# MLP weight pieces of a fused attention and MLP kernel: loads of 256 KB parts in place of whole pieces

## The chip, the cores and the metric

The kernel runs on one core of a Trainium2 chip. The metric is the device time of one execution in microseconds (us); medians are quoted. The engines are called PE (TensorE matmul), PEld (its weight loads), ACT (ScalarE), DVE (VectorE), POOL (GpSimd) and SP (SyncE, which here only issues DMAs). One program of 63,000 instructions is fully unrolled.

## The reference, cut to what matters

```python
def reference(A_x, A_wqkv, A_wo, B_x, B_w1, B_b1, B_w2, B_b2):   # S=2048, D=1024, 32 heads, F=3584, bf16
    x  = A_x
    xn = layernorm(x)
    s  = attention(xn, A_wqkv) @ A_wo                 # 32 heads of 32
    y  = layernorm(xn)
    g  = silu(gelu(y @ B_w1 + B_b1) @ B_w2 + B_b2)    # the MLP
    return x + s * g
```

## The kernel before

Attention is cut into 512 units. In each, PE makes the scores of four heads (line L591), ACT takes exp of them (L603), PE multiplies older ones with V and with ones (L620, L623). Into each unit one slice of other PE work is woven (L304): a projection, one w1 item (8 steps), or a quarter of a w2 item (7 steps). The MLP runs in 6 chunks of up to 352 tokens. For each chunk w1 and w2 are read again, in 7 w1 pieces of 1 MB and 4 w2 pieces of 1.75 MB, into two buffers `war0` and `war1` in turn. A w1 piece serves 4 units, a w2 piece 8.

A scheduler records every instruction with what it reads (`r`) and writes (`w`), and turns these into semaphore waits. An engine waits only for what its next instruction needs, so SP runs as far ahead of PE as free buffers let it (its largest sum of waits in the trace of before is for PE: 442.3 us in 29 waits at the w1 load, L363). It does so in program order.

```python
def load_piece(g):                       # called when the first item of piece g-1 starts
    ...                                  # cut: end test
    c, k = divmod(g, 11); s = g % 2
    if k < 7:                            # w1: 1 MB in one issue
        src = B_w1[:, k * 512:(k + 1) * 512].rearrange("(c p) f -> p c f", p=128)
        op("sync", lambda e: e.dma_start(w1v[s], src), w=[("war", s, 0)], dma=f"war{s}")
    else:                                # w2: 768 KB and 1 MB
        ...                              # cut: src
        op("sync", lambda e: e.dma_start(w2v[s][:, KLO:, :], src[:, KLO:, :]), w=[("war", s, 1)], dma=f"wah{s}")
        op("sync", lambda e: e.dma_start(w2v[s][:, 0:KLO, :], src[:, 0:KLO, :]), w=[("war", s, 0)], dma=f"war{s}")

# a w1 step on PE:   r=[("war", s, 0), "yTc"]
# a w2 step on PE:   r=[("war", s, 0 if f < KLO else 1), ("hT", f)]
# the main loop, one turn for a unit u:
#   scores; tanh; exp; P x V of unit u-2; [load_piece at a piece's start]; woven PE steps; DVE work and stores
```

The softmax here doesn't subtract the row's maximum and nothing guards it: scores larger than these inputs give would overflow.

Of the kernel before, what the change touches and what calls it, by code (L numbers as in the profile page):

```python
# [119 lines left out]
def bass_recurrent_scan__mha_block__mixer_channel_mlp__prompt_kernel(  # L120
# [38 lines left out]
    with ExitStack() as st:  # L159
        pg = _Prog(nc, st)  # L160
        op = pg.op

        def sb(name, shape, dt):
            return st.enter_context(nc.sbuf_tensor(name, list(shape), dt))
# [17 lines left out]
        hT = sb("hT", [128, FB, CW], BF16)  # L182
        yTc = sb("yTc", [128, DC, CW], BF16)
        war = [sb(f"war{i}", [128, FB * 256], BF16) for i in range(2)]
# [16 lines left out]
        w1v = [w[:, 0:DC * 512].rearrange("p (c f) -> p c f", c=DC) for w in war]  # L201
        w2v = [w[:, 0:FB * 256].rearrange("p (k n) -> p k n", k=FB) for w in war]
# [12 lines left out]
        def bank(i, lo=0, hi=512):  # L215
            return ps[:, i * 512 + lo:i * 512 + hi]

        def bankq(i, j, lo, hi):
            return ps[32 * j:32 * j + 32, i * 512 + lo:i * 512 + hi]
# [5 lines left out]
        for tb in range(NT):  # L225
            op("sync", lambda e, tb=tb: e.dma_start(xst[:, tb * D:(tb + 1) * D], x2[tb * 128:(tb + 1) * 128, :]),
               w=[("xst", tb)], dma=f"x{tb % 8}")
# [123 lines left out]
        cur = {"u": 0}  # L351
        cnt = {"w1": 0, "w2": 0, "piece": 0, "g": 0, "wo": 0, "store": 0}
        NPC = 11 * NCH
        KLO = 16

        def load_piece(g):
            if g >= NPC:
                return
            c, k = divmod(g, 11)
            s = g % 2  # L360
            if k < 7:
                src = B_w1[:, k * 512:(k + 1) * 512].rearrange("(c p) f -> p c f", p=128)
                op("sync", lambda e: e.dma_start(w1v[s], src), w=[("war", s, 0)], dma=f"war{s}")  # L363
            else:
                k -= 7
                src = B_w2[:, k * 256:(k + 1) * 256].rearrange("(k p) n -> p k n", p=128)
                op("sync", lambda e: e.dma_start(w2v[s][:, KLO:, :], src[:, KLO:, :]), w=[("war", s, 1)], dma=f"wah{s}")
                op("sync", lambda e: e.dma_start(w2v[s][:, 0:KLO, :], src[:, 0:KLO, :]), w=[("war", s, 0)], dma=f"war{s}")

        def load_y(c):  # L370
            t0, n = chunks[c]
# [3 lines left out]
        def w1_item(c, f):  # L375
            t0, n = chunks[c]
            g = 11 * c + f // 4
            s, fo = g % 2, (f % 4) * 128

            def pre():  # L380
                if f % 4 == 0:
                    load_piece(g + 1)

            def step(dc, bk):
                op("tensor", lambda e: mm4(e, lambda j: bankq(bk, j, 0, n),
                                           lambda j: w1v[s][:, dc, fo + 32 * j:fo + 32 * j + 32],
                                           yTc[:, dc, 0:n], dc == 0, dc == DC - 1),
                   r=[("war", s, 0), "yTc"], w=[("b", bk)])

            def fin(bk):  # L390
                m = cnt["w1"]
                cnt["w1"] += 1
                u = cur["u"]
                xb, ub, th = xb_t[m % NXB], u_t[m % NUB], th_t[m % NTH]
                kx, ku, kt = ("xb", m % NXB), ("ub", m % NUB), ("th", m % NTH)
                op("vector", lambda e: e.tensor_scalar(xb[:, 0:n], bank(bk, 0, n), b1T[:, f:f + 1], None, op0=ALU.add),  # L396
                   r=[("b", bk), "b1"], w=[kx])
                dve_tasks[u + 1].append(lambda: op(
                    "vector", lambda e: e.tensor_tensor(ub[:, 0:n], xb[:, 0:n], xb[:, 0:n], op=ALU.mult), r=[kx], w=[ku]))  # L399
                dve_tasks[u + 2].append(lambda: op(  # L400
                    "vector", lambda e: e.scalar_tensor_tensor(ub[:, 0:n], ub[:, 0:n], 1.0 / 0.044715, xb[:, 0:n], op0=ALU.add, op1=ALU.mult),  # L401
                    r=[kx, ku], w=[ku]))
                act_tasks[u + 3].append(lambda: op(
                    "scalar", lambda e: e.activation(th[:, 0:n], ub[:, 0:n], ACT.Tanh, scale=0.7978845608028654 * 0.044715),  # L404
                    r=[ku], w=[kt]))
                extra = [("xnb", i) for i in range(4)] + [("ybb", i) for i in range(4)] if c == 0 else []
                dve_tasks[u + 3].append(lambda: op(
                    "vector", lambda e: e.scalar_tensor_tensor(hT[:, f, 0:n], th[:, 0:n], 1.0, xb[:, 0:n], op0=ALU.add, op1=ALU.mult),  # L408
                    r=[kt, kx], w=[("hT", f)] + extra))
                if f == FB - 1 and c + 1 < NCH:  # L410
                    load_y(c + 1)
            return Item([lambda bk, dc=dc: step(dc, bk) for dc in range(DC)], fin, pre=pre)

        def w2_item(c, nb):
            t0, n = chunks[c]
            g = 11 * c + 7 + nb // 2
            s, no = g % 2, (nb % 2) * 128

            def pre():
                if nb % 2 == 0:  # L420
                    load_piece(g + 1)

            def step(f, bk):
                op("tensor", lambda e: mm4(e, lambda j: bankq(bk, j, 0, n),
                                           lambda j: w2v[s][:, f, no + 32 * j:no + 32 * j + 32],
                                           hT[:, f, 0:n], f == 0, f == FB - 1),
                   r=[("war", s, 0 if f < KLO else 1), ("hT", f)], w=[("b", bk)])

            def fin(bk):
                m = cnt["w2"]  # L430
                cnt["w2"] += 1
                u = cur["u"]
                zh, th, gs = zh_t[m % 2], th2_t[m % 2], gst[m % 2]
                kz, kt, kg = ("zh", m % 2), ("th2", m % 2), ("gst", m % 2)
                op("vector", lambda e: e.tensor_scalar(zh[:, 0:n], bank(bk, 0, n), 0.25, b2h[:, nb:nb + 1], op0=ALU.mult, op1=ALU.add),  # L435
                   r=[("b", bk), "b2"], w=[kz])
                act_tasks[u + 2].append(lambda: op(
                    "scalar", lambda e: e.activation(th[:, 0:n], zh[:, 0:n], ACT.Tanh), r=[kz], w=[kt]))  # L438

                def last():  # L440
                    op("vector", lambda e: e.scalar_tensor_tensor(gs[:, 0:n], th[:, 0:n], 1.0, zh[:, 0:n], op0=ALU.add, op1=ALU.mult),
                       r=[kt, kz], w=[kg])
                    op("sync", lambda e: e.dma_start(gT_d[nb * 128:(nb + 1) * 128, t0:t0 + n], gs[:, 0:n]),
                       r=[kg], w=[("gT", nb, c)], dma=f"gst{m % 2}")
                dve_tasks[u + 2].append(last)
            return Item([lambda bk, f=f: step(f, bk) for f in range(FB)], fin, parts=4, pre=pre)

        tail = {}
# [55 lines left out]
        for b in range(NT // 4):  # L504
# [14 lines left out]
            for i in range(4):  # L519
                run_now(v_item(0, 4 * b + i, ev="scalar"))  # L520
            run_now(qk_item(0, 0, 512 * b, 512, ev="scalar"))
        load_piece(0)
        load_y(0)


# [2 lines left out]
        for c in range(NCH):  # L528
            for f in range(FB):
                mlp.append([(w1_item(c, f), 0, DC)])  # L530
            for nb in range(DC):
                it = w2_item(c, nb)
                q = FB // it.parts
# [117 lines left out]
        u = 0  # L651
        while u < NU + 2 or state["qi"] < total or any(k >= u for k in list(act_tasks) + list(dve_tasks)):
            cur["u"] = u
            if u < NU:
                s_unit(u)
            for t in act_tasks.pop(u, ()):
                t()
            if u < NU:
                exp_unit(u)
            if 2 <= u < NU + 2:  # L660
                pv_unit(u - 2)
            if state["qi"] < total:
                qi = state["qi"]
                entry = flat[qi]
                state["qi"] += 1
                it, lo, hi = entry
                for hp, which in loads.pop(qi, ()):
                    if hp < HG // 2:
                        load_wq(hp, which)
                if lo == 0:  # L670
                    if it.pre:
                        it.pre()
                    if u >= NU + 2:
                        state["bank"] = tail_banks[(tail_banks.index(state["bank"]) + 1) % len(tail_banks)]
                for s in it.steps[lo:hi]:
                    s(state["bank"])
                for t in dve_tasks.pop(u, ()):
                    t()
                if hi == len(it.steps):
                    it.finish(state["bank"])  # L680
                if state["qi"] == q_end:
                    tail["xfree"] = pg.lists["tensor"][-1]
                    op("sync", lambda e: e.dma_start(wo_sb, A_wo.rearrange("(c p) n -> p c n", p=128)), w=["wo"], dma="wo",
                       after=[tail["xfree"]])
            for t in dve_tasks.pop(u, ()):
                t()
            u += 1
# [52 lines left out]
```

## Time and profile before

| | before |
|---|---|
| median time | 1173.8 us |
| span of the trace | 1170.1 us |
| PE busy, ACT busy | 93%, 90% |
| a unit with a w1 item / a w2 quarter (timeline, start to start) | about 2.07 / 1.92 us |
| DMA, mean | 111 GB/s |

From the page of the kernel before (busy us and share of the span; then the chain of waits that ended last, by engine and by line):

```profile
span 1170.1 us, 62673 instructions
...
PE 1093.0 (93%) x29696; PEld 688.6 (59%) x29696; DVE 599.5 (51%) x1327; ACT 1054.9 (90%) x1281; POOL 88.2 (8%) x116
...
q8 instruction: 232, 3.80, 1.3%
...
PE 50%; ACT 42%; DVE 4%; DMA 3%; issue 2%; POOL 0%; SPq 0%; POOLq 0%
```

PE and ACT share the chain. "issue" is time in which an engine waited for nothing that the profile shows. The 232 packets on queue 8 carry instructions, 16 KB each; they fit PE, whose trace has 59,474 instructions, about 232 times 256. The list of waits of the same kernel (us in total, times, longest) has little about weights:

```profile
ACT P L603 <- PE ps L591: 15.1, 18, 1.9
...
PE ps L304 <- issue: 12.2, 12, 1.8
...
PE ps L304 <- DMA war<-in_B_w_dram: 2.2, 1, 2.2
```

Weights are waited for once. But PE stood still before L304 12 times for 12.2 us with no visible reason, and ACT's exp waited for PE's scores 18 times. One of these places, PE in the timeline of before (start, length, engine, line; in brackets the idle time and what ended it), and SP around it:

```profile
356.03 0.28 PE L623 MATMUL ps<-P,ones 128*32 128x256 bf16 x4
356.14 0.62 PE L304 MATMUL ps<-hT,war 128*32 128x352 bf16 x11
358.59 0.91 PE L304 MATMUL ps<-hT,war 128*32 128x352 bf16 x17 [1.83 <-issue]
```

```profile
349.82 0.58 SPq L232 DMA_DIRECT2D wq<-in_A_wqkv_dram  x1
350.44 0.58 SPq L367 DMA_DIRECT2D war<-in_B_w_dram  x1
351.07 2.02 SPq L368 DMA_DIRECT2D war<-in_B_w_dram  x1
358.98 0.36 SPq L443 DMA_DIRECT2D gT_scratch<-gst  x1
```

PE halts in the middle of a w2 quarter, after 11 of 28 matmuls, and the trace shows nothing that it waits for. It goes on at 358.59 us. Just before, 1.75 MB of weights (and 512 KB of `wq`) were put into the DMA queue. The DMA packet records of the trace show the missing piece: the 16 KB instruction packet that belongs to PE's next block, if the 232 packets are counted off against the 232 blocks (defined below), starts at 356.30 us and takes 0.92 us. PE had entered the instruction block before at 351.57 us, 4.74 us earlier. When few or no data packets are about, such a packet starts 0.2 to 0.9 us after that moment (the 101 cases with at most 20 data packets within 1 us of it: quarters 0.22, 0.45, 0.85 us). Here it starts when most of the weight burst is over; the rest still moves at over 300 GB/s until about 358.5 us. Of the 34 late ones in this trace (defined below), 21 start at most 0.8 us before their burst falls under 200 GB/s, or just after; 11 start 1.6 to 3.9 us before it.

**How stalls are counted below.** PE's instructions (weight loads, matmuls and 82 semaphore and drain instructions) are numbered together in order of time. The long gaps lie at number 193 modulo 256. With 232 packets of 16 KB for 59,474 instructions we take these places as the ends of blocks of 256 instructions, one packet each. A *boundary stall* is a matmul within 20 ns of such a place that starts over 0.28 us after the matmul before it; its length is that distance less 0.11 us. Before 86 us (the prologue) none are counted. The trace has 28, together 22.2 us. A *late refill* is an instruction packet that starts over 2.2 us after PE entered the block before. (The prediction used a looser filter that gave 24 stalls and 20.8 us.) By this count the stall of the example is 2.04 us long. In the chain that ended last, the pause of the example is (start, length, what):

```profile
356.76 1.83 issue
```

### The profile page before, as it was taken

To read this page: it belongs to the slowest core of one execution; us is meant where nothing else is said; L and a number is where in the kernel's file an instruction comes from. 1 tells how busy PE (TensorE), PEld (TensorE's weight loads), DVE (VectorE), ACT (ScalarE), POOL (GpSimd) and SP (SyncE) were. 2 spreads that over 40 slices of the span, in tenths; PEclk is the share of its full clock that TensorE was granted. 3 is DMA by queue.
4 is the path that set the end of the run, shared out by engine and by line. 5 is a ranking of instruction groups with operands and counts; after the bars stand their busy time and mean duration, and the time that the engine had idled before them with its cause. 6 is when DMAs were issued, how large, how long until landed. Compare 5 with 4: busy or idle time off the path is not lost.

```text
span 1170.1 us, 62673 instructions
## 1 busy us (share of the span) xinstructions
PE 1093.0 (93%) x29696; PEld 688.6 (59%) x29696; DVE 599.5 (51%) x1327; ACT 1054.9 (90%) x1281; POOL 88.2 (8%) x116
## 2 busy tenths in 40 slices
PE   0789999999998999999999999999999999899998
PEld 0555665566655666556666665566655566566666
DVE  2817665146682254764226675136673246742468
ACT  0459999999999999999999999999999999999960
POOL 1810000000000000000000000000000000000000
PEclk9999999999999999999999999999999999999999
DMA  9243226512245320433422225522145321752756
GB/s 198 110 122 105 62 80 170 161 60 75 75 125 159 113 80 4 146 102 103 133 64 77 76 87 144 174 87 76 51 127 155 115 72 50 227 150 78 134 139 173
DMA packets 198481, 129.87 MB, mean 111 GB/s; under 512 B 41552, under 2 KB 189008, under 8 KB 198224
## 3 DMA queue, kind: packets, MB, share of 16 engines
q1 hardware_dynamic: 193584, 125.85, 36.8%
q8 instruction: 232, 3.80, 1.3%
q0 software_dynamic: 4640, 0.02, 0.6%
q14 instruction: 25, 0.20, 0.1%
HBM read 104.87 MB, written 12.58 MB: 100 GB/s over the span
## 4 chain that ended last, share of the span: by engine, by line
PE 50%; ACT 42%; DVE 4%; DMA 3%; issue 2%; POOL 0%; SPq 0%; POOLq 0%
ACT P L603 37%; PE ps L304 30%; PE ps L591 8%; PE ps L620 7%; PE ps L623 5%; ACT th L404 3%; DMA b2h<-in_B_b_dram 2%; ACT xnT L298 1%; DMA war<-in_B_w_dram 1%; DVE stats L247 1%; DVE xb L396 1%; ACT thz L438 1%; DVE u L399 0%; DVE u L401 0%; DVE hT L279 0%
## 5 line engine op out<-in xcount | busy, mean ns | idle before, releaser
L603 ACT ACTIVATE P<-ps 128x1024 bf16<-128x1024 f32 x1024 | 984.6, 1103 | 18.7 <-PE ps L591 15.1
L620 PE MATMUL ps<-P,VP 128*32 128x256 bf16 x4096 | 262.9, 278 | 1.1 <-issue 1.0
L623 PE MATMUL ps<-P,ones 128*32 128x256 bf16 x4096 | 258.3, 273 | 1.6 <-issue 1.6
L304 PE MATMUL ps<-hT,war 128*32 128x352 bf16 (+1 forms) x5376 | 230.2, 308 | 8.6 <-issue 7.1
L304 PE MATMUL ps<-yTc,war 128*32 128x352 bf16 (+1 forms) x5376 | 225.9, 308 | 10.6 <-issue 5.0
L591 PE MATMUL ps<-QT,KT 32*128 32x256 bf16 x4096 | 204.2, 273 | 9.1 <-ACT P L603 5.1
L304 PEld LDWEIGHTS ps<-yTc,war 128*32 128x32 bf16 x5376 | 139.3, 97 | 57.8 <-issue 9.6
L620 PEld LDWEIGHTS ps<-P,VP 128*32 128x32 bf16 x4096 | 107.8, 95 | 111.0 <-issue 98.8
L304 PEld LDWEIGHTS ps<-hT,war 128*32 128x32 bf16 x5376 | 141.7, 97 | 50.7 <-issue 9.5
L396 DVE TENSOR_SCALAR xb<-ps,b1T 128x352 f32<-128x352 f32 (+1 forms) x168 | 96.1, 572 | 131.1 <-PE ps L304 130.1
L591 PEld LDWEIGHTS ps<-QT,KT 32*128 32x128 bf16 x4096 | 61.0, 92 | 155.6 <-ACT P L603 87.6
L304 PE MATMUL ps<-xnT,wq 128*32 128x352 bf16 (+2 forms) x2944 | 131.1, 321 | 9.2 <-ACT xnT L298 8.8
L643 POOL TENSOR_TENSOR OT<-accs,rcs 128x256 bf16<-128x256 f32 x64 | 53.0, 828 | 1022.5 <-DVE rcs L641 1022.5
L435 DVE TENSOR_SCALAR zh<-ps,b2h 128x352 f32<-128x352 f32 (+1 forms) x48 | 27.5, 573 | 180.2 <-PE ps L304 180.2
L623 PEld LDWEIGHTS ps<-P,ones 128*32 128x32 bf16 x4096 | 110.0, 96 | 3.7 <-issue 2.3
L408 DVE SCALAR_TENSOR_TENSOR hT<-th,xb 128x352 bf16<-128x352 f32 (+1 forms) x168 | 85.8, 511 | 37.7 <-ACT th L404 34.2
L304 PEld LDWEIGHTS ps<-xnT,wq 128*32 128x32 bf16 x2944 | 73.9, 98 | 42.0 <-ACT xnT L298 8.1
L404 ACT ACTIVATE th<-u 128x352 f32<-128x352 f32 (+1 forms) x168 | 97.4, 580 | 0.4
L399 DVE TENSOR_TENSOR u<-xb 128x352 f32<-128x352 f32 (+1 forms) x168 | 87.2, 519 | 0.2
L401 DVE SCALAR_TENSOR_TENSOR u<-u,xb 128x352 f32<-128x352 f32 (+1 forms) x168 | 82.9, 493 | 0.0
L304 PE MATMUL ps<-wq,xnT 128*32 128x256 bf16 x2048 | 66.7, 277 | 0.0
L634 DVE COPY accs<-ps 128x256 f32<-128x256 f32 x64 | 27.2, 424 | 67.9 <-PE ps L623 67.9
(44 smaller groups left out, 504.7 us busy)
## 6 DMA issues: line engine op xcount, KB each, us to landing
war<-in_B_w_dram SPq DMA_DIRECT2D x66, 1024.0 KB, 5.4
war<-in_B_w_dram SPq DMA_DIRECT2D x24, 768.0 KB, 5.4
wq<-in_A_wqkv_dram SPq DMA_DIRECT2D x12, 512.0 KB, 6.3
OT<-in_A_x_dram SPq DMA_DIRECT2D x16, 256.0 KB, 6.2
y_scratch<-hT SPq DMA_DIRECT2D x16, 256.0 KB, 2.0
xnT<-in_A_x_dram SPq DMA_DIRECT2D x16, 256.0 KB, 3.9
out_dram<-wq SPq DMA_DIRECT2D x16, 256.0 KB, 2.5
gT_scratch<-gst SPq DMA_DIRECT2D x40, 88.0 KB, 1.7
```

Source lines behind the costliest of these rows:

```text
L304: ins = e.matmul(outs(j), lhsT=lhs(j), rhs=rhs, start=start, stop=stop, tile_position=(0, 32 * j), skip_group_check=True)
L396: op("vector", lambda e: e.tensor_scalar(xb[:, 0:n], bank(bk, 0, n), b1T[:, f:f + 1], None, op0=ALU.add), r=[("b", bk), "b1"], w=[kx])
L399: "vector", lambda e: e.tensor_tensor(ub[:, 0:n], xb[:, 0:n], xb[:, 0:n], op=ALU.mult), r=[kx], w=[ku]))
L401: "vector", lambda e: e.scalar_tensor_tensor(ub[:, 0:n], ub[:, 0:n], 1.0 / 0.044715, xb[:, 0:n], op0=ALU.add, op1=ALU.mult),
L404: "scalar", lambda e: e.activation(th[:, 0:n], ub[:, 0:n], ACT.Tanh, scale=0.7978845608028654 * 0.044715),
L408: "vector", lambda e: e.scalar_tensor_tensor(hT[:, f, 0:n], th[:, 0:n], 1.0, xb[:, 0:n], op0=ALU.add, op1=ALU.mult),
L435: op("vector", lambda e: e.tensor_scalar(zh[:, 0:n], bank(bk, 0, n), 0.25, b2h[:, nb:nb + 1], op0=ALU.mult, op1=ALU.add), r=[("b", bk), "b ...
L591: ins = e.matmul(bank(bks[j], kh * 256, (kh + 1) * 256), lhsT=KT[i2][32 * j:32 * j + 32, k0:k0 + 128], rhs=QT[i2][32 * j:32 * j + 32, qb * ...
L603: op("scalar", lambda e, p=p, sl=sl: e.activation(pb[:, 2 * p:2 * p + 2, :, :].rearrange("p a b q -> p (a b q)"), ps[:, sl * 1024:(sl + 1) ...
L620: e.matmul(bankq(ACC, j, 0, QW), lhsT=VP[vp][:, kb, vo + 32 * j:vo + 32 * j + 32], rhs=pb[:, j, kh, :], start=first, stop=False, tile_posi ...
L623: ins = e.matmul(bankq(ACC, j, QW, 2 * QW), lhsT=ones[:, 0:32], rhs=pb[:, j, kh, :], start=False, stop=last, tile_position=(0, 32 * j), sk ...
L643: op("gpsimd", lambda e: e.tensor_tensor(OT[:, hg, qb * QW:(qb + 1) * QW], a[:], rc[:], op=ALU.mult), r=[ka, kr], w=[("OT", hg, qb), ("xst ...
```

## The change

The intent is to soften the bursts: parts of 256 KB, "one in each unit". Every part has its own key and semaphore, so PE also waits for parts and not for pieces, and a part may overwrite its place as soon as the old part was read.

```diff
-                op("sync", lambda e: e.dma_start(w1v[s], src), w=[("war", s, 0)], dma=f"war{s}")
...
+        def load_sub(g, q):                                   # one part of 256 KB
+            if k < 7:
+                dst, lo, hi = w1v[s], 2 * q, 2 * q + 2
+            else:
+                dst, lo, hi = w2v[s], 4 * q, 4 * q + 4
+            op("sync", lambda e: e.dma_start(dst[:, lo:hi, :], src[:, lo:hi, :]), w=[("war", s, q)], dma=f"war{s}{q}")
+
+        def load_piece(g):
+            if k <= 7:  subs = [0, 1, 2, 3]                   # (shortened)
+            else:       subs = [0, 1, 2, 3, 4, 5, 6]
+            for i, q in enumerate(subs):
+                sp_tasks[cur["u"] + i].append((load_sub, g, q))
+            if k == 4:                                        # upper half of the first w2 piece
+                for i, q in enumerate((4, 5, 6)):
+                    sp_tasks[cur["u"] + 1 + i].append((load_sub, g + 3, q))
-                   r=[("war", s, 0), "yTc"], w=[("b", bk)])
+                   r=[("war", s, dc // 2), "yTc"], w=[("b", bk)])
-                   r=[("war", s, 0 if f < KLO else 1), ("hT", f)], w=[("b", bk)])
+                   r=[("war", s, f // 4), ("hT", f)], w=[("b", bk)])
+                for fn, *a in sp_tasks.pop(u, ()):            # in the main loop, before the woven steps
+                    fn(*a)
```

## The prediction

> **What bounds the kernel.** The page: TensorE matmul (PE) busy 93%, ScalarE (ACT) 90% of 1170.1 us; the chain of waits is PE 50%, ACT 42%. Each of the 512 attention units carries one slice of projection or MLP work; it takes about 2.07 us with a w1 item, 1.92 us with a w2 quarter (timeline). Weights are not late: the list of waits has one PE wait for `war`, 2.2 us at 1011 us, behind the 2 MB load of wo. Traffic doesn't slow compute: exp takes 1107 ns (mean) when over 250 GB/s move, 1106 ns when almost nothing does.
>
> **What the bursts cost.** The chain has 17 "issue" pieces over 0.15 us after 86 us, together 15.2 us (1.83 us at 356.8, 1.50 at 222.7, 1.48 at 756.0). The 15 stalls that I checked lie at the same place of PE's instruction stream, number 193 modulo 256, and end about 2.3 us after the start of a 16 KB packet on the instruction queue. [...] in quiet time a refill packet starts about 0.3 us after PE enters the block before; beside a weight burst 2.4 to 4.7 us after, near the burst's end, and PE stands still. Of 24 such stalls (20.8 us on PE), 16 had a `war` load in flight; some others follow `wq` or wo loads, which stay.
>
> **What the change does.** Bytes and packet sizes stay. A w1 piece, 1 MB in one issue, becomes 4 parts; a w2 piece, 768 KB + 1 MB, becomes 7; 90 loads become 336. Despite the name, nothing ties a part to its unit: SyncE runs ahead, and a part waits only for the last reader of the same part of the old piece (and for `gst` stores ahead in the queue). So w1 parts go out almost back to back. A 256 KB issue costs SyncE about 0.46 us (the x loads at the start); a burst drains at about 330 GB/s (packet records), 0.78 us a part. Estimate: backlog after the fourth part 4 x 0.78 - 3 x 0.46 = 1.7 us, against 3.2 us for a whole w1 piece and over 4.5 us for a w2 piece. A refill tolerates about 2 us. So most `war` stalls should vanish. w2 parts spread better: they come free over four units, and the stores split them.
>
> Costs: some 246 more landing waits on PE, with data long there: near 0. SyncE has idle time. Parts 2 and 3 of a chunk's second w1 piece sit behind a store: perhaps 0.5 us of PE wait, five times. Gain besides: up to 1 us at the wait of 1011 us, as part 0 lands first.
>
> **Sum.** The stalls are on the chain: at most 15 us. I leave 3 to 4 us for `wq`/wo stalls and new coincidences: gain about 11 us, 0.9%. Predicted 1163 us, 8 in 10 within 1157 to 1170. Faster by over 2%: 0.03; within 2%: 0.95; slower: 0.02.
>
> **What would show it.** "Issue" pieces of the chain fall from 15 us to below 5; stalls at block boundaries from 24 to below 10, survivors beside wq/wo; exp and matmul durations unchanged; PE waits for `war` below 4 us; part issues about 0.46 us apart, not 2 us.
>
> **What would make it wrong.** If refills wait for burst bytes in any form, stalls stay: 1170. If SyncE's in-order queue delays late parts, PE waits for `war` appear. If removed stalls only uncover ACT or DVE, the gain halves.

"A refill tolerates about 2 us" is an estimate that the trace of before bears out, counted here for all 225 refills whose block ends after the prologue: of 188 that started at most 2.0 us after PE had entered the block before, only four were followed by a stall (four small ones, together 1.4 us, which have the same length in both kernels and stay in the best version); of 21 at over 2.0 and up to 3.0 us, 8 were, none longer than 0.43 us; of 16 at over 3.0 us, all were, by 0.57 to 2.04 us. PE took 4.66 us for a block (median), and after the 23 late refills with a stall it went on 2.2 to 2.6 us after the packet's start (median 2.32). The difference, 4.66 - 2.32 = 2.3 us, is our estimate of what a refill can lose.

## The result, and the profile after

| | before | after |
|---|---|---|
| median time, first comparison | 1173.76 us | 1154.94 us |
| median time, control beside the later experiments | 1173.84 us | 1156.15 us |
| ratio, first / control | | 0.9841 [0.9812, 0.9870] / 0.9847 [0.9830, 0.9864] |
| span of the trace | 1170.1 us | 1153.3 us |
| boundary stalls | 28, 22.2 us | 9, 5.2 us |
| late refills | 34 | 13 |
| PE waits for `war` | 2.2 us | 0.7 us |

A ratio is the mean time of one kernel's fast runs over the mean of the other's of the same rounds, so it is not quite the ratio of the quoted medians; brackets hold the 95% interval. The kernel became about 18 us faster, 11 had been forecast, and 1155 lies below the range of 1157 to 1170.

The same lines of the page after:

```profile
span 1153.3 us, 62919 instructions
...
PE 1090.9 (95%) x29696; PEld 687.7 (60%) x29696; DVE 600.7 (52%) x1327; ACT 1050.9 (91%) x1281; POOL 88.5 (8%) x116
...
q8 instruction: 232, 3.80, 1.3%
...
ACT 58%; PE 35%; DVE 4%; DMA 2%; issue 1%; SPq 0%; POOL 0%; POOLq 0%
```

and of the list of waits after:

```profile
ACT P L618 <- PE ps L606: 3.5, 8, 1.2
...
PE ps L304 <- issue: 2.6, 4, 1.0
...
PE ps L304 <- DMA war<-in_B_w_dram: 0.7, 3, 0.3
```

Busy times hardly moved. PE's unexplained idle time before L304 went from 12.2 to 2.6 us, and ACT's waits for the scores from 15.1 to 3.5. The chain now runs mostly through ACT (42% before, 58% after). The place of the example, the same unit in the timeline after, PE and SP:

```profile
353.82 0.28 PE L638 MATMUL ps<-P,ones 128*32 128x256 bf16 x4
353.93 1.22 PE L304 MATMUL ps<-hT,war 128*32 128x352 bf16 x28
355.09 0.29 PE L606 MATMUL ps<-QT,KT 32*128 32x256 bf16 x4
```

```profile
347.87 0.58 SPq L232 DMA_DIRECT2D wq<-in_A_wqkv_dram  x1
348.49 5.59 SPq L365 DMA_DIRECT2D war<-in_B_w_dram  x6
```

The 28 matmuls run through. Six parts still leave in one row of 5.6 us, not one in each unit of 1.9 us. Over the whole trace, 65% of successive part issues are under 0.8 us apart, with a median of 0.51 us among these.

Unit by unit, the two traces differ by more than 0.3 us in 23 of the 511 unit-to-unit distances. Those 23 sum to 18.1 us, all others to -1.4 us. The seven largest (2.13, 1.82, 1.80, 1.72, 1.65, 1.36 and 1.32 us) are units with a boundary stall in the trace before. The start of the first unit (85.6 us) and the tail after the start of the last one (39.6 us) are the same in both. So the gain consists of stalls that are gone, and of 1.5 us less waiting for `war`; nothing else shown here got faster.

### The profile page after: what moved, and what is told of

It is laid out like the page before. It is cut to its first block, busy times and chain, and to the rows that moved or that the text cites. A ratio compares the mean times of both kernels' runs of the same rounds, so it can differ in the third digit from the quotient of the medians.

```text
span 1153.3 us, 62919 instructions
## 1 busy us (share of the span) xinstructions
PE 1090.9 (95%) x29696; PEld 687.7 (60%) x29696; DVE 600.7 (52%) x1327; ACT 1050.9 (91%) x1281; POOL 88.5 (8%) x116
## 4 chain that ended last, share of the span: by engine, by line
ACT 58%; PE 35%; DVE 4%; DMA 2%; issue 1%; SPq 0%; POOL 0%; POOLq 0%
ACT P L618 52%; PE ps L304 22%; PE ps L606 5%; PE ps L635 5%; ACT th L418 3%; PE ps L638 3%; DMA b2h<-in_B_b_dram 1%; ACT thz L452 1%; ACT xnT L298 1%; DMA war<-in_B_w_dram 1%; DVE stats L247 1%; DVE xb L410 1%; DVE u L413 0%; DVE u L415 0%; DVE hT L279 0%
## 5 line engine op out<-in xcount | busy, mean ns | idle before, releaser
L304 PE MATMUL ps<-yTc,war 128*32 128x352 bf16 (+1 forms) x5376 | 225.5, 308 | 6.3 <-DVE xb L410 2.9
L304 PE MATMUL ps<-hT,war 128*32 128x352 bf16 (+1 forms) x5376 | 228.0, 308 | 1.5 <-DVE xb L410 1.5
L304 PEld LDWEIGHTS ps<-yTc,war 128*32 128x32 bf16 x5376 | 138.2, 97 | 54.5 <-DVE xb L410 6.0
L304 PEld LDWEIGHTS ps<-hT,war 128*32 128x32 bf16 x5376 | 140.8, 97 | 42.4 <-DVE xb L410 2.4
L304 PE MATMUL ps<-xnT,wq 128*32 128x352 bf16 (+2 forms) x2944 | 131.5, 321 | 9.2 <-ACT xnT L298 8.8
L418 ACT ACTIVATE th<-u 128x352 f32<-128x352 f32 (+1 forms) x168 | 101.5, 604 | 0.1
L304 PEld LDWEIGHTS ps<-xnT,wq 128*32 128x32 bf16 x2944 | 73.8, 98 | 42.6 <-ACT xnT L298 8.1
L304 PE MATMUL ps<-wq,xnT 128*32 128x256 bf16 x2048 | 67.4, 279 | 0.0
```

The lines of the kernel that those rows point to most:

```text
L304: ins = e.matmul(outs(j), lhsT=lhs(j), rhs=rhs, start=start, stop=stop, tile_position=(0, 32 * j), skip_group_check=True)
L418: "scalar", lambda e: e.activation(th[:, 0:n], ub[:, 0:n], ACT.Tanh, scale=0.7978845608028654 * 0.044715),
```

## The experiments

**Theory**, to be tested. PE's next block of instructions comes by DMA (the 232 packets of 16 KB on queue 8). A large issue of data delays it (4.74 us in the example), and PE runs dry at the block's end (2.04 us). That the length of the queue of bytes ahead is what counts is the model, here and in the expectations: the traces show late starts, not a queue. **Rivals:** (a) finer waits let weights leave or be used earlier; (b) the spreading over units does it; (c) the moved bytes as such slow PE. All experiments are edits of the kernel after, unless told otherwise, and all gave correct results.

| run | edit in a word | median us | ratio to before | span | boundary stalls | late refills | PE waits for `war`, us |
|---|---|---|---|---|---|---|---|
| before | | 1173.8 | | 1170.1 | 28, 22.2 us | 34 | 2.2 |
| before_again | none | 1173.73 | 1.0002 [0.9977, 1.0027] | 1175.2 | 29, 24.7 us | 32 | 2.1 |
| after | the change | 1154.94 | 0.9841 [0.9812, 0.9870] | 1153.3 | 9, 5.2 us | 13 | 0.7 |
| after_again | the change | 1156.15 | 0.9847 [0.9830, 0.9864] | 1155.1 | 11, 7.5 us | 15 | 0.0 |
| e1_at_once | parts not put off | 1157.18 | 0.9854 [0.9840, 0.9867] | 1154.6 | 13, 6.3 us | 15 | 0.7 |
| e2_whole_waits | waits of whole pieces | 1157.25 | 0.9858 [0.9842, 0.9873] | 1154.6 | 10, 4.2 us | 17 | 0.0 |
| e3_halves | parts of 512 KB | 1163.09 | 0.9910 [0.9889, 0.9931] | 1159.6 | 19, 10.3 us | 33 | 1.8 |
| e4_idle_burst | + 1 MB idle copies | 1186.02 | 1.0107 [1.0089, 1.0126] | 1183.1 | 45, 34.0 us | 58 | 1.8 |
| e9_idle_parts | + the same in parts | 1165.39 | 0.9929 [0.9899, 0.9958] | 1161.0 | 11, 6.1 us | 17 | 4.9 |
| e5_paced | part waits for its unit | 1155.79 | 0.9843 [0.9827, 0.9860] | 1154.1 | 7, 2.4 us | 7 | 3.1 |
| e6_wq_wo_parts | wq, wo in parts too | 1153.85 | 0.9830 [0.9813, 0.9847] | 1151.2 | 7, 3.1 us | 11 | 0.4 |
| e7_all_paced | e5 and e6 | 1153.43 | 0.9831 [0.9811, 0.9851] | 1152.2 | 5, 1.7 us | 2 | 3.3 |
| e8_two_a_unit | e7, w1 parts by twos | 1150.75 | 0.9804 [0.9782, 0.9826] | 1149.0 | 4, 1.4 us | 3 | 0.0 |

### The unit in which a part is written

```diff
-                sp_tasks[cur["u"] + i].append((load_sub, g, q))
+                load_sub(g, q)
```
(and the same for the upper half of the first w2 piece.)

> All parts of a piece are issued at the piece's start, none is put off to a later unit. Theory (size of an issue counts, the unit it is written in does not, since SyncE runs ahead): ratio to the kernel before 0.980 to 0.989, as for the change, 4 to 7 PE stalls at block boundaries. Rival (the parts help because they are spread over units): much of the gain goes, ratio 0.992 or more, 12 or more stalls.

The ratio is 0.9854, within the range. The stalls are 13 with 6.3 us. Their number is the one that the rival had forecast (12 or more), but they take no more time than the control's 7.5 us, and the time of the kernel is that of the change. Rival (b) falls in the form "the unit in which the code puts the part matters".

### The finer waits

```diff
-            op("sync", ... w=[("war", s, q)], dma=f"war{s}{q}")
+            op("sync", ... w=[("war", s, q)], dma=f"war{s}{q}", after=[last step of the whole old piece])
-                   r=[("war", s, dc // 2), "yTc"]
+                   r=[("war", s, q) for q in range(4)] + ["yTc"]       # w2: all 7
```

> The loads are split as in the change, but the waits are those of whole pieces: every part waits for the last reader of the whole old piece, and PE's steps wait for all parts. Theory (only the split of the burst counts, because the instruction refill queues behind it): ratio 0.980 to 0.990, up to 3 us lost to parts that now leave closer together. Rival (the gain comes from the finer waits, parts leaving and being used earlier): ratio 0.994 or more, as before.

With the waits of whole pieces in both directions the ratio is 0.9858; the interval overlaps that of the change. Rival (a) falls. Splitting the issue is what counts. Its span is 1.3 us longer than that of the change with 1.0 us less of stalls; its first unit began 2.0 us later.

### Parts of 512 KB

```diff
-                dst, lo, hi = w1v[s], 2 * q, 2 * q + 2
+                dst, lo, hi = w1v[s], 2 * q, 2 * q + 4          # (shortened) q in (0, 2); w2: q in (0, 2, 4, 6)
```

> Parts of 512 KB (two to a w1 piece, four to a w2 piece). Theory (queue ahead of a refill against about 2 us that a refill can wait): backlog after the second part about 2 x 1.56 - 0.5 = 2.6 us, so some stalls come back: 8 to 14 of them, ratio 0.986 to 0.993. Rival (any split is as good, what counts is that the first part lands early): ratio 0.981 to 0.986.

The 2 us are those of the prediction, with the counts given there. The ratio is 0.991, inside the range, with 10.3 us of stalls between the 5.2 of parts and the 22.2 of whole pieces. The number of stalls (19) was put too low (8 to 14). Size matters step by step, as a queue would have it; that it is a queue is argued, not shown.

### A burst that nobody waits for, whole and in parts

```diff
+        def load_junk(k, g):            # at each piece, in the unit of its last part; device memory to device memory
+            op("sync", lambda e: e.dma_start(junk_d[g % 2] ..., B_w1[...] ...), w=[("junk", g % 2)], dma=f"jk{g % 2}",
+               after=[pg.lists["tensor"][-1]])
```
e9 cuts the same copy into four of 256 KB, tied to four units.

> The change, plus a useless copy of 1 MB within device memory at each piece, in one issue, that no instruction waits for. Theory (refills queue behind any large burst): the stalls come back, 20 or more of them, over 18 us of PE, ratio 0.995 or more, with few PE waits for weights. Rival (the gain came from how weights are waited for): ratio stays at 0.982 to 0.988.

> The same useless bytes as in e4_idle_burst, but in four copies of 256 KB tied to four units of PE. Theory (the length of the queue ahead of a refill counts, not the bytes moved): well under half of the stall time of e4, at most 16 us against 34, ratio 0.987 to 0.999. Rival (the added traffic as such slows PE, or takes refill bandwidth): ratio near that of e4, 1.006 or more.

With the whole burst the time is 1186 us and the stalls are 34.0 us. PE and SP of the timeline of e4:

```profile
197.75 0.61 SPq L371 DMA_DIRECT2D junk<-in_B_w_dram  x1
198.40 1.36 SPq L366 DMA_DIRECT2D war<-in_B_w_dram  x2
```

```profile
203.62 0.76 PE L305 MATMUL ps<-hT,war 128*32 128x352 bf16 x13
205.73 0.78 PE L305 MATMUL ps<-hT,war 128*32 128x352 bf16 x15 [1.35 <-issue]
```

PE halts within a quarter as it did before the change, behind a copy that has nothing to do with its operands. In parts, the same bytes leave 6.1 us of stalls, about what the change has. So rival (c) falls for the stalls: what matters is not the bytes, but that they leave in one piece. e9 changes two things against e4, the size of the issue and the spacing, and does not tell them apart. e9 is still about 10 us slower than the change. Of the 7.7 us between the two spans, 4.2 us are added PE waits for `war` (4.9 against 0.7; our guess is that true parts now come behind idle ones, which is not shown), and 0.9 us are stalls. Most of the rest is a halved PE clock: the clock records of e9 have half clock for 3.4 us from 992.5 us and again from 1006.1 us, and the three units there take 2.5 us more than the same units of the change.

### Pacing that is real

```diff
+               after=[pg.lists["tensor"][-1]] if paced else [])     # the part waits for PE to reach its unit
```

> Each part now truly waits for PE to reach its unit, so parts leave about 2 us apart. Theory: backlog never over 0.8 us from weights alone, so only stalls beside the loads of wq and wo are left (about 3 of the 6): 1 to 2 us faster than the change, ratio 0.980 to 0.984. Rival (the change's name is already true, or the spacing doesn't matter): no difference, same stalls. If late parts are waited for, PE waits for war of 3 us or more and ratio over 0.986.

This expectation failed. The median distance of successive part issues is now 2.04 us and the stalls fall to 2.4 us, as the theory says, but the time does not: the list of waits of this run has a new entry.

```profile
PE ps L304 <- DMA war<-in_B_w_dram: 3.1, 6, 1.0
```

Where no projection stands between w1 items, a piece lasts four units, and a fourth part that leaves in the fourth unit lands too late. The stall was turned into a wait of about the same size.

### wq and wo in parts; everything paced; two parts to a unit

```diff
-   wq: one load of 512 KB per matrix                +   two of 256 KB, keys ("wq", t3, half), one in each unit, paced
-   wo: one load of 2 MB                             +   eight of 256 KB, keys ("wo", hc), one in every second unit, paced
```
e7 joins this with e5. e8 then has:
```diff
             for i, q in enumerate(subs):
+                i = i // 2 if k < 7 else i              # w1 parts leave two to a unit
```

> The change, with the loads of wq (512 KB) and wo (2 MB) also in parts of 256 KB, paced by PE's units. Theory: the stalls near 217, 470 and 995 us and the wait for war behind wo go, about 3 us: ratio 0.979 to 0.983. Rival (those stalls have another cause): ratio as the change, 0.984.

> Both together: weights, wq and wo in parts of 256 KB, each paced by PE. Theory: no more than 2 stalls at block boundaries, ratio 0.977 to 0.982, about 1150 us. Rival: no better than the change, 0.984.

> As e7, but the four parts of a w1 piece leave two to a unit of PE, so the last is there before the piece is due; backlog at most about 2 x 0.78 - 0.46 = 1.1 us. Theory (e7 bought the last stalls with 3.3 us of waits for late parts): stalls stay at 6 or fewer, PE waits for war under 1 us, 1 to 3 us faster than e7: ratio 0.979 to 0.983. If it is as e7 (0.983), those waits were off the critical path.

e6 is at 0.983, the edge of its range, and its interval overlaps the control's. The stalls near 217, 470 and 995 us are gone; two of about 0.7 us came, at 269.7 and 664.0 us. e7 reached 0.9831, just outside the range, with 3.3 us of waits for `war`. Its count of 5 includes the four that never go, which the 2 that had been expected did not allow for. e8 removes these waits: nothing but the four small stalls is left, no PE wait for `war`, and the median is 1150.75 us. It beats both kernels: 23 us under before, and its interval does not touch the control's (which ran in another set, each beside the kernel before), though it overlaps a little with that of the first comparison. From the page of e8, the span and the chain by engine, in which "issue" has become 0%:

```profile
span 1149.0 us, 62938 instructions
...
ACT 64%; PE 30%; DVE 4%; DMA 2%; issue 0%; POOL 0%; POOLq 0%
```

### A second trace of the kernel before

> The kernel before, for a second trace. The forecast took 15.2 us, the issue pieces of the chain, as the most that could be won; the stalls on PE in that trace added up to 20.8 us by the count used then. If stall time is what sets the span, a trace of a run 2 us longer has about 2 us more of it: span 1171 to 1174 us and stalls of 22 to 26 us by the stricter count (matmuls at block boundaries; 22.2 us in the first trace). Ratio 0.998 to 1.002.

The stalls, 24.7 us, lie in the range; the span, 1175.2 us, does not: it is 5.1 us longer than the first, with 2.5 us more of stalls. The other part is a halved clock, seen in the windows view of this run (us, busy time and instructions of each engine, then the granted PE clock, the DMA share and GB/s):

```profile
1012.00:1016.00 4.00, 2.17 (x64) 1.15 (x52) 3.59 (x8) 4.00 (x6) 0.85 (x1) 0.98 0.93 303
1016.00:1023.00 7.00, 5.98 (x100) 3.33 (x104) 1.99 (x5) 2.93 (x5) 0.00 (x0) 0.52 0.78 254
```

While PE stood still for 2.13 us in a wait for `war`, at the place where `war` follows the 2 MB load of wo, the clock fell, and the clock records show half clock for 6.8 us; the two units there took 5.12 and 3.44 us, against 4.21 and 1.86 in the first trace, together 2.5 us more. The pause lasted from 1014.89 to 1017.02 us, and half clock began at 1015.9, 1.0 us into it. The first trace of before had a pause of 2.16 us at the same place and kept its clock, so the length of the pause alone does not decide; what does is open. Of the 13 traces three have half clock between 990 and 1030 us: this one, e4 and e9. The two traces of the kernel after do not.

### All traces together

A least-squares line through the 13 spans gives span = 1148.1 + 0.96 x boundary stalls + 1.15 x PE waits for `war` (us), with no trace over 2.5 us off it. Stalls from 1.4 to 34 us cost their own length, nearly one for one. The factor of the waits is less sure: without e9, which also has the half clock, it is 0.80 (that of the stalls 0.98).

## Why the prediction was wrong

- *"PE stands still at block boundaries because refills come late beside weight bursts."* Right. e4 (58 late refills, 34.0 us of stalls) against e9 (17 and 6.1 us) shows it without any change of the weights' own path (that the packet comes "near the burst's end" holds for most late refills, not for the example above).
- *"Nothing ties a part to its unit."* Right: median 0.51 us between the parts of a row (0.46 forecast), and e1 shows that the unit written in the code makes no difference.
- *"A refill tolerates about 2 us; four parts make a queue of 1.7 us."* The first half fits the trace of before (4 of 188 refills within 2.0 us were followed by a stall, all 16 over 3.0 us were). The second, an estimate, is consistent with e3, where 2.6 us of estimated queue brought part of the stalls back (10.3 us, against 5.2). The survivors fit too: the stall at 824.7 us follows seven parts in 3.2 us, where a w1 piece and the upper half of a w2 piece leave together. This case the forecast had not seen; seven parts are more than four.
- *"Costs near 0; PE waits for `war` below 4 us."* Right: 0.7 us.
- *"The stalls are on the chain: at most 15 us. I leave 3 to 4 us ...: gain about 11 us."* **This is the step that failed, and of its two terms the first.** 15 was the sum of the chain's "issue" pieces, 15.2 us. The stalls that could go were 20.8 us (22.2 less the 1.4 that never go). Those left after the change are 5.2 - 1.4 = 3.8 us, just what had been left for them. 20.8 - 3.8 = 17.0 us, and the span fell by 16.8. That these two agree so closely is in part luck: the waits for `war` also fell by 1.5 us, and the units without a large difference lost 1.4 us. The chain is short for two reasons. It counts a pause only from the modelled end of the last matmul; the same 17 pauses measure 18.3 us from start to start, 0.19 us more in each. And it leaves out the other 11, 3.9 us in all, of which 1.4 us are the four that never go. The pause of the example is 1.83 us in the chain and 2.04 us from start to start. The forecast had the larger number, 20.8 us on PE, and took the smaller one as the cap.
- The remaining 1 to 2 us between 16.8 (spans) and 17.7 to 18.8 (medians) come from the trace: the first trace of before was of a run of 1171.9 us, below the median of 1173.8; the second, of 1177.1 us, has 24.7 us of stalls and the half clock. The half clock seems to give little to the medians: of the 29 runs of before beside the experiments, 13 have a mean clock of 0.994 or less, as the three traces with half clock do, and their median is 1174.0 us; that of the other 16 is 1173.5.

What stays open: where the refill is held up. The trace shows when its packet starts, not when it was asked for, nor what it waited for in between. That a refill waits behind the bytes queued before it is a model that forecast most of these runs; no run shows the queue itself.

## What to carry to other kernels

In this long unrolled program PE's instructions came by DMA as the data did (232 packets of 16 KB), and with large single issues the engine with the most instructions stood still at block ends for 22.2 us of 1170 before the change, and for 34.0 us of 1183 in e4. Look for pauses with no releaser at equal distances in the instruction stream, and add them up from start to start on the limiting engine; don't take a chain's rounding of them as the cap. The cure here was to keep each burst short, and to issue every part just early enough that the last one isn't waited for (e8: 1.4 us of stalls, no PE wait for `war`). Four parts of 256 KB (an estimated queue of 1.7 us, from 0.78 us of draining and 0.46 us of issue a part) were mostly harmless, with 5.2 us of stalls, and two of 512 KB (2.6 us by the same estimate) were not, with 10.3 us. Parts of 256 KB made this kernel about 18 us faster, parts of 512 KB 10.6.
